# Attention and an MLP on one core: W1 loads in 2 KB rows, and a batch's head transposes moved from TensorE to DMA

## Chip, cores and metric

The kernel runs on one core of one Trainium2 chip. The metric is the device time of one execution in microseconds. Before the change the median of three runs is 740.92 us (740.89 to 741.25).

## What is computed

Grouped-query attention (8 batches, 16 query heads on 4 key/value heads, 384 tokens, head size 64) gives x of 384 x 1024 per batch. A residual MLP with affine norms follows:

```
scores = scale * q @ k^T;  attn = softmax(scores);  x = attn @ v      (heads side by side)
a1  = alpha1 * x + beta1
u   = x + lam * (w_tok @ a1)
a2  = alpha2 * u + beta2
out = u + lam * (relu(a2 @ w_ch1) @ w_ch2)        w_ch1: 1024 x 4096, w_ch2: 4096 x 1024
```

## The kernel before

**Stages.** Batch 0's attention runs first (`side(0)`). Then `main(0)` runs the MLP of batch 0, and the attention of batch 1 is woven into it; `main(1)` runs the MLP of batch 1 with the attention of batch 2. These two are the plain passes. Then `pair(0)` to `pair(2)` run the MLPs of the other six batches two by two, with sums and differences of blocks in place of some of the products. The attention of each later batch is woven into the stage ahead of it.

**The order is written by hand.** All five instruction streams are in the order in which the program calls them (`manual_schedule`, L836). `main` and `pair` are generators: they yield 0 in the first matrix product and 1 in the second, and the driver (L1011 to L1026) counts these units and calls what `put(ps, phase, unit, ...)` has planned for each. A plan entry therefore fixes a place in each engine's own order. An engine waits only for semaphores of data that it needs, or of a buffer that must be free.

**First product of a plain pass** (L524 to L547). W1 is taken in 16 chunks of 256 columns (`CW` = 2 column tiles of 128) over all 1024 rows of K. They go through a ring of `RING` = 6 slots in SBUF. `load_w1` (L183) issues one transfer from GpSimd's queue (POOL), which also casts f32 to bf16: 1 KB source rows, 512 KB written. `order1` is 0, 8, 1, 9, 2, 10, ...; batch 1 goes through it backwards. For each column tile `nt` there are eight matmuls (L531) over `dt`, the eight parts of K. Then ACT or VectorE (DVE) applies bias and ReLU and writes `hT` (L540, L542); `exps`, set by the exponentials (L290), decides which of the two does it. When a chunk's two tiles are done its slot is freed and the chunk six places on is loaded (L545). PSUM has two banks for these products. In batch 0 the first four column tiles (`FIRST`: 0, 1, 16, 17) are computed early, inside `side(0)` (`h_part`, L223), since `a2` is not complete yet.

**W2** is held whole in SBUF during the plain passes. Three of its sixteen parts (512 KB, 2 KB source rows, L189) are loaded early and 13 after batch 0's last W1 load (L549), all on POOL's queue. Behind them come the keys, queries and values of batch 2 (`load_next(2)`). POOL has at most eight transfers under way. The second product (L569) goes over the column tiles in the order of the first; the first two output tiles are each run to three quarters before they are finished.

**Heads.** Attention needs q and k with head dimension on partitions. For batch 1 TensorE transposes them (`k_transpose` L255, `q_transpose` L265) at units 9, 24, 28, 32, 36 and 40 of `main(0)`'s first product, and DVE copies the result out of PSUM (L257, L267). For batches 2 to 7 DMA transposes issued from SP do it (`flip_k` L172, `flip_q` L176). `kT` and `qT` have one buffer each, and so have the raw keys (`k2s`) and queries (`qrs`).

**The other parts that the prediction's steps touch.** On SP: rows of parameters (`load_row_set`, L924), the spill of x (L243), the transposes of `a2` (L362), and the stores of batch 0 (L518). On PE: the scores (L279, three calls at a time in `scores3`), attention times values (L315) and token mixing (L340). `scores3(0)` of batch 1 stands at unit 0 of `main(0)`'s second product and reads the keys and the queries of heads 0 to 3. `late` holds back the last exponential of some `scores3` until after the next `av` (L408).

**The end** (L767 to L796, `last` and `o == 4`). The last of seven products goes through the first half of its 16 K parts for token tiles 0, 1, 2 and then through the second half for 0, 1, 2. Token tile 2 is in two PSUM pieces, 384 and 128 columns wide. Two DVE operations on each finished piece (L794, L795) and a store from SP (L796) follow.

Of the kernel before, what the change touches and what calls it, by code (L numbers as in the profile page):

```python
# [12 lines left out]
def kernel(  # L13
# [21 lines left out]
    nc = tc.nc  # L35
# [13 lines left out]
    P = 128  # L49
# [7 lines left out]
    CW = 2  # L57
# [57 lines left out]
    def by_tok(ap):  # L115
        return ap.rearrange("(p st) d -> p st d", st=NST)
# [64 lines left out]
    w1_slots, w1_free = {}, list(range(RING))  # L181

    def load_w1(c):  # L183
        w1_slots[c] = w1_free.pop(0)
        nc.gpsimd.dma_start(out=w1[:, w1_slots[c]], in_=w1src[:, :, c * CW * P:(c + 1) * CW * P])  # L185

    def load_w2(dw, r, h):
        cs = slice(dw * 512, (dw + 1) * 512)
# [23 lines left out]


    early = {}
    FIRST = (0, 1, NH, NH + 1)

    def h_part(nts, dts):
        for nt in nts:
            if nt % 2 == 0 and nt not in early:
                t = bank([P, 2, 512], "sc", "h")  # L220
                early[nt], early[nt + 1] = t[:, 0], t[:, 1]
            for dt in dts:
                nc.tensor.matmul(out=early[nt][:, :S + 1], lhsT=w1[:, w1_slots[nt // CW], dt, nt % CW * P:(nt % CW + 1) * P],  # L223
                                 rhs=a2Ts[0][:, dt, :S + 1], start=(dt == 0), stop=(dt == NDT - 1))


# [2 lines left out]
    def side(b):  # L229
# [175 lines left out]
        def av(p):  # L405
            av_piece(p, 0)
            av_piece(p, 1)
            while late:  # L408
                late.pop(0)()

        def tok_flip(p):
            tok(p)
# [18 lines left out]
        if not first:  # L431


            turns = {}
            if b == 1:
                turns = {5: [(to_all, 3, 0, 0), (load_row_set, 1, 1, 0)], 7: [(to_all, 3, 1, 1), (load_row_set, 2, 0, 1)],
                         9: [(k_transpose, 0)], 12: [(to_all, 1, 0, 2)], 14: [(to_all, 1, 1, 0), (load_row_set, 2, 1, 0)],
                         17: [(scale_beta,)], 20: [(to_all, 2, 0, 1)], 22: [(to_all, 2, 1, 0)],
                         24: [(q_transpose, 0, 2, "av")], 28: [(k_transpose, 2)]}
                for i in range(3):  # L440
                    turns[32 + 4 * i] = [(q_transpose, 2 + 2 * i, 2, "av")]
            if (b - NPL) // 2 > 0:
                at = {}

                def put(k, *m):
                    at.setdefault(k, []).append(m)

                for j in range(6):
                    put((0, 6, 12, 21, 26, 31)[j], scores3, j, j in (2, 5))
                for p in range(NP):  # L450
                    put((4, 10, 14, 18, 24, 29, 33, 35)[p], av, p)
                    put((8, 15, 17, 22, 27, 32, 36, 38 if b % 2 else 39)[p], tok_flip, p)
                    if by_pe(p):
                        put((36, 39, 41)[p - NP + 3], turn, p)
                return turns, at
            return turns, {
                0: [(scores3, 0)], 4: [(av, 0)], 6: [(scores3, 1)], 8: [(tok_flip, 0)], 11: [(av, 1)],
                13: [(scores3, 2, True)], 15: [(av, 2)], 16: [(tok_flip, 1)], 18: [(tok_flip, 2)], 19: [(av, 3)],
                21: [(scores3, 3)], 23: [(tok_flip, 3)], 25: [(av, 4)], 27: [(scores3, 4)], 29: [(tok_flip, 4)],
                31: [(av, 5)], 33: [(scores3, 5, True)], 35: [(av, 6), (tok_flip, 5)], 37: [(av, 7)],  # L460
                38: [(tok_flip, 6)], 41: [(tok_flip, 7)],
                **{39 + 4 * i - i // 2 * 2: [(turn, p)] for i, p in enumerate((5, 6, 7)) if by_pe(p)}}
# [20 lines left out]
            for f, *a in at.get(i, []):  # L483
                add(f, *a)
        for f, *a in ((tok, 4), (ut, 3), (h_part, (0, 1), range(3)), (av, 7), (a1, 7), (tok, 5), (ut, 4), (h_part, (0, 1), (3,)),
                      (tok, 6), (h_part, (16, 17), range(4)), (ut, 5), (tok, 7), (h_part, FIRST, (4,)), (ut, 6),
                      (h_part, FIRST, (5,)), (ut, 7), (h_part, FIRST, (6,)), (h_part, FIRST, (7,))):
            add(f, *a)
        return us
# [18 lines left out]
            f(**a)  # L508


    order1 = [c for g in range(NCH // 2) for c in (g, g + NCH // 2)]

    def store(b, ms, dw, o):
# [6 lines left out]
    def main(b):  # L520
        a2T = a2Ts[b]
        n = S + 1 if b == 0 else S

        seq = order1[::-1 if b % 2 else 1]  # L524
        for i, c in enumerate(seq):
            for j in range(CW):
                nt = c * CW + j
                begun = b == 0 and nt in early
                ps = early[nt] if begun else bank([P, 512], "mm", "h")
                for dt in range(0 if begun else NDT):  # L530
                    nc.tensor.matmul(out=ps[:, :n], lhsT=w1[:, w1_slots[c], dt, j * P:(j + 1) * P],  # L531
                                     rhs=a2T[:, dt, :n], start=(dt == 0), stop=(dt == NDT - 1))
                    if dt == 3:
                        yield 0
                c1 = bias1[:, nt:nt + 1]
                if b == 0:
                    evac("DVE" if nt % 2 else "ACT")(out=c1, in_=ps[:, S:n])
                exps[0] -= 1
                if (b or nt % 2 == 0) and exps[0] < 0:
                    nc.scalar.activation(out=hT[:, nt, :], in_=ps[:, :S], func=RELU, bias=c1)  # L540
                else:
                    nc.vector.tensor_scalar(out=hT[:, nt, :], in0=ps[:, :S], scalar1=c1,  # L542
                                            scalar2=0.0, op0=ADD, op1=mybir.AluOpType.max)
                yield 0
            if i + RING < NCH:  # L545
                w1_free.append(w1_slots.pop(c))
                load_w1(seq[i + RING])  # L547

            if b == 0 and i == NCH - RING:  # L549
                for dw, r, h in [(0, 1, 1)] + [(0, r, h) for r in (2, 3) for h in range(2)] + [  # L550
                        (1, r, h) for r in range(4) for h in range(2)]:
                    load_w2(dw, r, h)
                load_next(2)
        nts = [c * CW + j for c in seq for j in range(CW)]
        units = [(dw, ms) for dw in range(NDW) for ms in range(NST)]
        runs = [(k, 0, NNT) for k in range(len(units))]
        if b == 0:
            most = 3 * NNT // 4
            runs[:2] = [(k, lo, hi) for lo, hi in ((0, most), (most, NNT)) for k in range(2)]
        open_ps = {}  # L560
        for k, lo, hi in runs:
            dw, ms = units[k]
            cs = slice(dw * 512, (dw + 1) * 512)
            if lo == 0:
                open_ps[k] = bank([P, 512], "mm", "ch")
            ps = open_ps[k]
            for i in range(lo, hi):
                nt = nts[i]
                nc.tensor.matmul(out=ps, lhsT=hT[:, nt, ms * P:(ms + 1) * P],  # L569
                                 rhs=w2[:, row(nt)[0], row(nt)[1], cs], start=(i == 0), stop=(i == NNT - 1))  # L570
                if i % 4 == 3 and i < NNT - 1:
                    yield 1
            if hi < NNT:
                continue
            o = obuf[:, k % 2 * 512:(k % 2 + 1) * 512]
            nc.vector.tensor_tensor(out=o, in0=ps, in1=lam_t[:, cs], op=MUL)
            if b == 0:
                nc.vector.tensor_tensor(out=o, in0=o, in1=xs[0][:, ms, cs], op=ADD)
            store(b, ms, dw, o)
            yield 1  # L580
# [89 lines left out]
    def pair(i):  # L670
# [95 lines left out]
        where = {2: (0, 0), 3: (0, 1), 7: (1, 1), 4: (1, 0)}  # L766
        for k, o in enumerate(PLACE2):  # L767
            whole = not last and o != 4
            for h in range(1 if whole else 2):
                for ms in range(NST):  # L770
                    if o == 4 and not last and 1 < 3 * h + ms < 5:
                        sum_w1(0, (5, 7, 6)[3 * h + ms - 2])
                    if last and (o, h) in ((6, 1), (7, 0)):
# [7 lines left out]
                        X[ms] = c_banks(ms)  # L781
                        pairs["held"] = ms == NST - 1
                    upto = NH if whole else 8 * h + 8
                    for (c0, c1, x), t in ((c, t) for c in X[ms] for t in range(8 * h, upto)):
                        slot, rhs = w2_slots[i, 4 * k + t // 4], w2_at[i, 4 * k + t // 4]
                        nc.tensor.matmul(out=x, lhsT=hid[:, t, LEFT2[o], ms * P:(ms + 1) * P],  # L786
                                         rhs=rhs[:, t % 4 * 512 + c0:t % 4 * 512 + c1],
# [4 lines left out]
                        if last and o == 4 and t == NH - 1:  # L792
                            e, v = ends[ms][:, c0:c1], spare(ms).bitcast(f32)[:, c0:c1]
                            tt(out=v, in0=x, in1=lam_t[:, c0:c1], op=MUL)  # L794
                            tt(out=e, in0=e, in1=v, op=ADD)  # L795
                            nc.sync.dma_start(out=by_tok(out[b0 + 1])[:, ms, c0:c1], in_=e)  # L796
                        if t % 4 == 3 and t < upto - 1 and c1 == 512:
                            q = 4 * ms + t // 4
                            if whole and o in (2, 6) and q in (2, 5, 8, 10):
# [36 lines left out]
    with tc.manual_schedule(engines=order):  # L836
# [104 lines left out]
        nc.gpsimd.dma_start(out=wtok_in, in_=moe_w_tok.rearrange("(p tt) s -> p tt s", tt=NST))  # L941
        load_q4(3)
        place_k(0, 0, (0,))
        load_w1(order1[0])
        load_w1(order1[1])
        place_k(0, 1)
        scale_rows(1, nc.gpsimd)
        split(1, 2, None, nc.gpsimd)
        for c in order1[2:RING]:
            load_w1(c)  # L950

        load_q(1)
# [27 lines left out]
        turns, at = side(1)  # L980
        put_all(0, 0, turns)
        put_all(0, 1, at)
        put_flips(0, 1, 2, (34, 36, 37, 42, 43))

        put(0, 1, 45, load_next, 3)
# [71 lines left out]
```

## Time and profile before

| what | value |
|---|---|
| runs | 740.92 us median (740.89, 740.92, 741.25) |
| profiled execution | 740.56 us |
| its span, first to last instruction | 738.8 us |
| mean granted TensorE clock | 0.999 |
| TensorE (PE) busy | 731.5 us, 99% |
| VectorE (DVE) busy | 516.9 us, 70% |
| ScalarE (ACT) busy | 324.1 us, 44% |
| GpSimd (POOL) busy | 163.5 us, 22% |
| queue q0 (POOL's transfers) | 64.60 MB |
| queue q1 (SP's transfers) | 85.39 MB |

The profile gives one execution, in microseconds from the span's first instruction. Each group of instructions has its line, engine, operation and tiles; "idle before" is the time in which its engine did nothing ahead of it, with what ended that. The chain of work follows the last instruction back to what released it, step by step. The DMA view gives the packets and bytes of each queue, for the span or for a window of it; sizes are those written. The time to landing of a transfer is counted from its issue.

### The profile page before, as it was taken

Reading aid. Unit: us, or ns where it says so; the run is one execution under the profiler, and the core shown is the slowest. Engines: PE = TensorE matmul, PEld = TensorE weight load, DVE = VectorE, ACT = ScalarE, POOL = GpSimd, SP = SyncE. Lnnn points to the kernel's source line nnn. Section 1 sums busy time; section 2 is a strip of 40 time slices with the busy share of each in tenths; the row PEclk is TensorE's granted clock in tenths of the full one; section 3 lists DMA queues with packets and bytes.
Section 4 is the critical chain, followed back from the end, with each engine's and each line's share of the span. In section 5 each row is a group of like instructions: output and inputs, shape, how many; then the busy total and the mean of one; then the engine's idle time right before and its main releaser. Section 6 shows DMA issues by size and latency. Waiting matters only on the chain.

```text
span 738.8 us, 14511 instructions
## 1 busy us (share of the span) xinstructions
PE 731.5 (99%) x5769; PEld 418.8 (57%) x5769; DVE 516.9 (70%) x995; ACT 324.1 (44%) x467; POOL 163.5 (22%) x211
## 2 busy tenths in 40 slices
PE   8999999999999999999999999999999999999997
PEld 5866555566555566655555566655555566654444
DVE  7763366467587889749777988847968988762354
ACT  7632431444333566653334366664343266660000
POOL 9434221420000232211013244020002222000011
PEclk9999999999999999999999999999999999999999
DMA  9999999999899999999989999998989999937965
GB/s 184 194 202 200 207 209 175 185 191 199 204 258 281 177 218 212 268 249 205 297 197 197 202 149 191 204 246 198 274 236 172 211 127 145 172 117 261 293 182 103
DMA packets 218017, 151.32 MB, mean 205 GB/s; under 512 B 88660, under 2 KB 197060, under 8 KB 217948
## 3 DMA queue, kind: packets, MB, share of 16 engines
q0 software_dynamic: 120304, 64.60, 66.6%
q1 hardware_dynamic: 97100, 85.39, 42.9%
q8 instruction: 45, 0.74, 0.4%
q10 hardware_dynamic: 544, 0.39, 0.2%
q14 instruction: 24, 0.20, 0.1%
HBM read 154.84 MB, written 38.27 MB: 261 GB/s over the span
## 4 chain that ended last, share of the span: by engine, by line
PE 95%; DVE 2%; DMA 1%; ACT 0%; issue 0%; DVEq 0%
PE C L786 30%; PE X L722 17%; PE h L531 10%; PE ch L569 10%; PE Y L722 8%; PE sc L279 5%; PE Z L722 4%; PE sc L315 4%; PE sc L340 3%; DMA ops<-a 1%; PE h L223 1%; PE tok L340 1%; PE av L315 0%; PE warm L841 0%; PE tp L265 0%; ACT hT L288 0%
## 5 line engine op out<-in xcount | busy, mean ns | idle before, releaser
L288 ACT ACTIVATE es<-sc 128x1024 bf16<-128x1024 f32 x126 | 121.4, 1023 | 155.9 <-PE sc L279 144.8
L786 PE MATMUL C<-w,arena 128*128 128x512 bf16 (+2 forms) x744 | 168.0, 372 | 0.0
L786 PEld LDWEIGHTS <-arena 128*128 128x128 bf16 x1040 | 94.8, 98 | 100.5 <-issue 5.1
L727 ACT ACTIVATE hT<-X,bias 128x384 f32<-128x384 f32 x144 | 83.7, 581 | 61.6 <-PE X L722 54.9
L722 PEld LDWEIGHTS <-w 128*128 128x128 bf16 x768 | 75.1, 98 | 50.0
L516 POOL DMA_DIRECT2D out_dram<-hT x33 | 28.7, 871 | 284.3 <-DVE hT L687 106.3
L569 PE MATMUL ch<-arena,hT 128*128 128x512 bf16 x384 | 90.8, 379 | 0.0
L185 POOL DMA_DIRECT2D w<-in_moe_w_ch_dram x68 | 62.8, 964 | 98.4 <-PE X L722 34.4
L531 PE MATMUL h<-ops,w 128*128 128x384 bf16 (+1 forms) x480 | 83.3, 327 | 0.8 <-DVE hT L542 0.7
L722 PEld LDWEIGHTS <-pad 128*128 128x128 bf16 x576 | 56.4, 98 | 37.2
L722 PE MATMUL X<-ops,w 128*128 128x384 bf16 x384 | 70.2, 326 | 0.0
L722 PE MATMUL X<-ops,pad 128*128 128x384 bf16 x384 | 70.2, 326 | 0.0
L786 PE MATMUL C<-pad,arena 128*128 128x512 bf16 (+2 forms) x296 | 69.9, 373 | 0.0
L531 PEld LDWEIGHTS <-w 128*128 128x128 bf16 x480 | 45.4, 98 | 30.4 <-issue 2.7
L569 PEld LDWEIGHTS <-hT 128*128 128x128 bf16 x384 | 34.8, 98 | 36.8 <-issue 2.5
L347 DVE TENSOR_TENSOR xr<-sc,xr 128x384 f32<-128x384 f32 x56 | 30.9, 552 | 23.4 <-PE sc L340 23.4
L315 PEld LDWEIGHTS <-es 128*128 128x128 bf16 x1008 | 38.2, 97 | 12.4
L340 PEld LDWEIGHTS <-wtokT 128*128 128x128 bf16 x576 | 37.5, 98 | 11.8 <-DVE a L330 0.8
L279 PE MATMUL sc<-qT,kT 64*128 64x384 bf16 (+2 forms) x576 | 42.0, 272 | 0.8 <-DVE xr L323 0.3
L320 DVE RECIPROCAL rinv<-sc 128x6 f32<-128x6 f32 x56 | 10.7, 192 | 44.3 <-PE sc L315 44.1
L315 PE MATMUL sc<-v,es 128*128 128x65 bf16 x1008 | 39.8, 193 | 0.0
L722 PE MATMUL Z<-ops,w 128*128 128x384 bf16 x192 | 39.0, 326 | 0.0
(138 smaller groups left out, 911.0 us busy)
## 6 DMA issues: line engine op xcount, KB each, us to landing
w<-in_moe_w_ch_dram POOLq DMA_DIRECT2D x68, 512.0 KB, 10.3
w<-w2s SPq DMA_DIRECT2D x60, 512.0 KB, 4.3
pad<-w2s SPq DMA_DIRECT2D x24, 512.0 KB, 8.1
out_dram<-xr SPq DMA_DIRECT2D x56, 192.0 KB, 6.1
out_dram<-hT POOLq DMA_DIRECT2D x33, 256.0 KB, 5.7
arena<-in_moe_w_ch_dram POOLq DMA_DIRECT2D x16, 512.0 KB, 20.0
w2s<-arena SPq DMA_DIRECT2D x28, 256.0 KB, 5.0
q_raw<-in_q_dram POOLq DMA_DIRECT2D x28, 192.0 KB, 10.4
```

The costliest lines, as they stand in the source:

```text
L185: nc.gpsimd.dma_start(out=w1[:, w1_slots[c]], in_=w1src[:, :, c * CW * P:(c + 1) * CW * P])
L279: nc.tensor.matmul(out=sc[:, hh, k % 4:k % 4 + n], lhsT=kT[r, 2 * p // G, BLK[hh][sk], :], rhs=qT[r, p, st:st + n, :], start=True, stop=True)
L288: nc.scalar.activation(out=e, in_=sc, func=EXP, scale=scale_qk)
L315: nc.tensor.matmul(out=av[:, hh, sq, :], lhsT=ess[k // 4][:, m % 2, k % 4, :], rhs=vb[:, sk, hk, :], start=(sk == 0), stop=(sk == NST - 1))
L340: nc.tensor.matmul(out=ps[:, tt, :], lhsT=wtokT[:, st, tt * P:(tt + 1) * P], rhs=a1s[p][:, st, :], start=(st == 0), stop=(st == NST - 1 an ...
L347: nc.vector.tensor_tensor(out=u, in0=ps, in1=u, op=ADD)
L516: nc.gpsimd.dma_start(out=at, in_=o, accum_op=ADD)
L531: nc.tensor.matmul(out=ps[:, :n], lhsT=w1[:, w1_slots[c], dt, j * P:(j + 1) * P], rhs=a2T[:, dt, :n], start=(dt == 0), stop=(dt == NDT - 1))
L569: nc.tensor.matmul(out=ps, lhsT=hT[:, nt, ms * P:(ms + 1) * P], rhs=w2[:, row(nt)[0], row(nt)[1], cs], start=(i == 0), stop=(i == NNT - 1))
L722: nc.tensor.matmul(out=ps, lhsT=tb[g, o][:, dt, e * P:(e + 1) * P], rhs=opb(LEFT1[o])[:, dt], start=(o in (1, 2, 7) and dt == 0), stop=(dt ...
L727: nc.scalar.activation(out=snap[o, e], in_=ps, func=IDENT, bias=hi if o == 5 else lo)
L786: nc.tensor.matmul(out=x, lhsT=hid[:, t, LEFT2[o], ms * P:(ms + 1) * P], rhs=rhs[:, t % 4 * 512 + c0:t % 4 * 512 + c1], start=((not last o ...
```

## The change

1. In batch 0, and in the first half of batch 1, W1 is taken in chunks of 512 columns over half of K's rows: 2 KB source rows, again 512 KB written, in the same six slots. Four column tiles now use two slots (`half`, `w1_of`), and both are freed and loaded again after the four. `order0` is column group 0, 4, 1, 5, 2, 6, 3, 7, each with its two halves of K. Batch 1 goes through groups 7, 3, 6, 2 and then through chunks 11, 3, 10, 2, 9, 1, 8, 0 of the old form. `FIRST` becomes 0, 1, 2, 3. The 13 loads of W2 and `load_next(2)` stand after 20 column tiles and not after 22.
2. Batch 1's keys and queries are transposed by DMA: `flip_k(1)` and two `flip_q` at units 50, 54, 58 of `main(0)`'s first product, two more at units 3 and 9 of its second. TensorE's six groups of transposes are gone.
3. After held-back exponentials have run, `exps` is 1 and not 2.
4. At the end, token tile 2 is left out of the first half and run over all 16 K parts last; the store of its 128-column piece is issued by ACT.

```diff
     def load_w1(c):
-        w1_slots[c] = w1_free.pop(0)
-        nc.gpsimd.dma_start(out=w1[:, w1_slots[c]], in_=w1src[:, :, c * CW * P:(c + 1) * CW * P])
+        w1_slots[c] = slot = w1_free.pop(0)
+        if isinstance(c, tuple):
+            src = w1src[:, c[1] * NDT // 2:(c[1] + 1) * NDT // 2, c[0] * 512:(c[0] + 1) * 512]
+            nc.gpsimd.dma_start(out=half(slot), in_=src)
+        else:
+            nc.gpsimd.dma_start(out=w1[:, slot], in_=w1src[:, :, c * CW * P:(c + 1) * CW * P])
+
+    def half(slot):
+        return w1[:, slot].rearrange("p a c -> p (a c)").rearrange("p (a c) -> p a c", a=NDT // 2)
+
+    def w1_of(nt, dt):
+        g = nt // 4, dt // (NDT // 2)
+        if g in w1_slots:
+            return half(w1_slots[g])[:, dt % (NDT // 2), nt % 4 * P:(nt % 4 + 1) * P]
+        return w1[:, w1_slots[nt // CW], dt, nt % CW * P:(nt % CW + 1) * P]
...
-    FIRST = (0, 1, NH, NH + 1)
+    FIRST = (0, 1, 2, 3)
...
             while late:
                 late.pop(0)()
+                exps[0] = 1
...
-                         9: [(k_transpose, 0)], 12: [(to_all, 1, 0, 2)], 14: [(to_all, 1, 1, 0), (load_row_set, 2, 1, 0)],
-                         17: [(scale_beta,)], 20: [(to_all, 2, 0, 1)], 22: [(to_all, 2, 1, 0)],
-                         24: [(q_transpose, 0, 2, "av")], 28: [(k_transpose, 2)]}
-                for i in range(3):
-                    turns[32 + 4 * i] = [(q_transpose, 2 + 2 * i, 2, "av")]
+                         12: [(to_all, 1, 0, 2)], 14: [(to_all, 1, 1, 0), (load_row_set, 2, 1, 0)],
+                         17: [(scale_beta,)], 20: [(to_all, 2, 0, 1)], 22: [(to_all, 2, 1, 0)]}
...
-                      (tok, 6), (h_part, (16, 17), range(4)), (ut, 5), (tok, 7), (h_part, FIRST, (4,)), (ut, 6),
+                      (tok, 6), (h_part, (2, 3), range(4)), (ut, 5), (tok, 7), (h_part, FIRST, (4,)), (ut, 6),
...
+    order0 = [(q + h, i) for q in range(4) for h in (0, 4) for i in range(2)]
...
-        seq = order1[::-1 if b % 2 else 1]
-        for i, c in enumerate(seq):
-            for j in range(CW):
-                nt = c * CW + j
+        seq = order1[7::-1] if b else order0
+        if b:
+            seq = [(q, i) for q in (7, 3, 6, 2) for i in range(2)] + seq
+        to_load, nts = seq[RING:], []
+        for c in [c for c in seq if c not in order0 or not c[1]]:
+            mine = [(c[0], 0), (c[0], 1)] if c in order0 else [c]
+            for nt in range(4 * c[0], 4 * c[0] + 4) if c in order0 else range(CW * c, CW * c + CW):
+                nts.append(nt)
...
-            if i + RING < NCH:
-                w1_free.append(w1_slots.pop(c))
-                load_w1(seq[i + RING])
-
-            if b == 0 and i == NCH - RING:
+            fresh = bool(to_load)
+            for m in mine if fresh else ():
+                w1_free.append(w1_slots.pop(m))
+                load_w1(to_load.pop(0))
+
+            if b == 0 and fresh and not to_load:
...
+            tail = last and o == 4
             for h in range(1 if whole else 2):
-                for ms in range(NST):
+                for ms in range(NST - (tail and not h)):
...
-                    for (c0, c1, x), t in ((c, t) for c in X[ms] for t in range(8 * h, upto)):
+                    for (c0, c1, x), t in ((c, t) for c in X[ms]
+                                           for t in range(0 if tail and ms == NST - 1 else 8 * h, upto)):
...
-                            nc.sync.dma_start(out=by_tok(out[b0 + 1])[:, ms, c0:c1], in_=e)
+                            (nc.scalar if c0 else nc.sync).dma_start(out=by_tok(out[b0 + 1])[:, ms, c0:c1], in_=e)
...
-        load_w1(order1[0])
-        load_w1(order1[1])
+        load_w1(order0[0])
+        load_w1(order0[1])
...
+        put_flips(0, 0, 1, (50, 54, 58))
+        put(0, 1, 3, flip_q, 1, 4, 2)
+        put(0, 1, 9, flip_q, 1, 6, 2)
```

More of the change, by code (lines that the diff above doesn't have):

```diff
@@ L222, in h_part @@
             for dt in dts:
-                nc.tensor.matmul(out=early[nt][:, :S + 1], lhsT=w1[:, w1_slots[nt // CW], dt, nt % CW * P:(nt % CW + 1) * P],
+                nc.tensor.matmul(out=early[nt][:, :S + 1], lhsT=w1_of(nt, dt),
                                  rhs=a2Ts[0][:, dt, :S + 1], start=(dt == 0), stop=(dt == NDT - 1))
@@ L530, in main @@
                 for dt in range(0 if begun else NDT):
-                    nc.tensor.matmul(out=ps[:, :n], lhsT=w1[:, w1_slots[c], dt, j * P:(j + 1) * P],
+                    nc.tensor.matmul(out=ps[:, :n], lhsT=w1_of(nt, dt),
                                      rhs=a2T[:, dt, :n], start=(dt == 0), stop=(dt == NDT - 1))
@@ L553, in main @@
                 load_next(2)
-        nts = [c * CW + j for c in seq for j in range(CW)]
         units = [(dw, ms) for dw in range(NDW) for ms in range(NST)]
@@ L948 @@
         split(1, 2, None, nc.gpsimd)
-        for c in order1[2:RING]:
+        for c in order0[2:RING]:
             load_w1(c)
```

## The prediction

> **What bounds the kernel now.** First the page's engine and chain lines:
>
> ```profile
> span 738.8 us, 14511 instructions
> PE 731.5 (99%) x5769; PEld 418.8 (57%) x5769; DVE 516.9 (70%) x995; ACT 324.1 (44%) x467; POOL 163.5 (22%) x211
> PE 95%; DVE 2%; DMA 1%; ACT 0%; issue 0%; DVEq 0%
> ```
>
> TensorE is the bound nearly everywhere, at a granted clock of 1.00 in every stage. A matmul removed from it is time won, and a wait added to it is time lost. The waits of PE come to 3.2 us in the whole span, and none of them is for a transfer:
>
> ```profile
> PE warm L841 <- DVE wtokT L844: 1.5, 1, 1.5
> PE h L531 <- DVE hT L542: 0.7, 1, 0.7
> ...
> ```
>
> That PE does not wait for transfers does not mean that transfers have room. The table of stages gives the DMA share above 1.2 from 10 to 130 us, so I read the DMA view in three windows there: 50 to 60 us (W1 in 1 KB source pieces, 512 B written), 72 to 84 us (W2 in 2 KB pieces, 1 KB written), and 93.5 to 95.5 us (W2 beside a DMA transpose from SP).
>
> ```profile
> DMA packets 3898, 1.98 MB, mean 198 GB/s; under 512 B 60, under 2 KB 3896, under 8 KB 3896
> ```
> ```profile
> DMA packets 2480, 2.48 MB, mean 206 GB/s; under 512 B 76, under 2 KB 2479, under 8 KB 2479
> ```
> ```profile
> q0 software_dynamic: 315, 0.31, 92.1%
> q1 hardware_dynamic: 313, 0.08, 29.9%
> ```
>
> W1 moves at 198 GB/s and W2 at 206: the load queue is saturated and the piece size is worth 4%. In the third window the two queues share the engines packet by packet, 315 to 313. So a transpose, in packets of 256 B (0.08 MB / 313), lets W2 through at 157 GB/s, 76% of its rate.
>
> **Slack of the W1 loads.** Number batch 0's sixteen loads in order of issue. Loads 7 to 16 are issued at 36.84 to 59.41 us; adding each one's time to landing, they land at 46.6, 49.3, 52.1, 54.8, 57.3, 60.1, 62.7, 65.4, 68.0, 70.6, one per 2.67 us. W2's next seven land one per 2.55 us, from 70.6 to 85.9. The PE timeline gives the consumption:
>
> ```profile
> 40.63 0.50 PE L255 MATMUL tp<-ident,k 128*128 128x128 bf16 x6
> 40.96 9.96 PE L531 MATMUL h<-ops,w 128*128 128x385 bf16 x60
> 50.76 0.50 PE L265 MATMUL tp<-ident,q_raw 128*128 128x128 bf16 x6
> ```
>
> Sixty matmuls take 50.76 - 40.96 = 9.80 us, 163 ns each, 1.31 us for a column tile of eight. L531 begins at 36.71, so load 7 is needed at 36.71 + 8 x 1.31 + 0.33 = 47.5 (landed 46.6), load 8 at 50.1 (49.3), load 16 at 72.6 (70.6). The slack is 0.8 to 2 us: PE is fed just in time.
>
> **Part 1, the second batch's heads.** Gone from PE: 2 groups on L255 and 4 on L265 of six transposes, each group 40.96 - 40.63 = 0.33 us: **-1.97 us**, all on the path. Their six VectorE copies of 0.55 us go too and are worth nothing, as DVE idles before each L537 there. Added on SP: one flip_k and four flip_q. SP works in its own order and each waits only for its data. Ahead of them stands the last row load of the first stage:
>
> ```profile
> 41.34 4.36 SPq L924 DMA_DIRECT2D rows<-in_moe_alpha_dram  x2
> ```
>
> The keys of batch 1 are converted by 36.4 (L160), the queries have landed by 35, and kT and qT were last read for batch 0 before 27 us. So the places 50, 54 and 58 in the plan hold nothing back: flip_k and the first three flip_q are issued from 45.8 on, one after another. The row load issued by 45.7 reached DVE at 49.73 (its shuffle L928 waited for it), so I let the flips' first packets move at 50 us. They carry 12 + 3 x 6 = 30 blocks of 128 x 128 in bf16, 32 KB or 128 packets each: 3840 packets at 157 per us, 24.5 us, until 74.5. Over that time the loads' spacing grows from 2.55 to 2.55 x 206 / 157 = 3.34 us. The flips themselves are in time: flip_k ends at 59.8, then 64.7, 69.6, 74.5, and the first scores come with the second matmul product after 75. The fourth flip_q stands on SP behind the first spill (86.64) and T of L362 (87.38, landed after 9.3), some 13 us before its scores (107.8).
>
> **Part 2, W1 in halves of four column tiles.** The loads gain (2.67 - 2.55) each, so load 7 lands 7 x 0.12 = 0.8 to 0.9 earlier, at 45.7. But four tiles now need two loads: loads 7 and 8 are both wanted at tile 20, at 36.71 + 8 x 1.31 = 47.2 and, for the second half of K, 4 x 0.163 later, 47.8. Before, load 8 was wanted at 50.1. It lands at 45.7 + 2.55 = 48.25: a new wait of 0.47, even without flips. With flips (3.34 from 50 us on) loads 10, 12, 14, 16 land at 53.9, 60.6, 67.2, 73.9; wanted, each 5.23 + the waits so far after the one before, at 53.5, 59.2, 65.8, 72.5. **Waits: 0.47 + 0.43 + 1.43 + 1.43 + 1.43 = 5.2 us**, all on PE, with nothing to hide them: the products of W1 are all that PE has there. What is queued behind the waiting matmul on PE is the whole rest of the kernel. Loads are issued by POOL after the last reader of a slot, two at a time; load 15 can be issued at 58.7 and would move at 66, so issue is not the limit. POOL's time per load falls (0.87 to about 0.74, as L189's same shape), hidden.
>
> [...]
>
> W2 behind: its loads land some 3.7 us later. The tightest (columns 0 to 511, rows 8 to 11, second half of NNT) landed at 78.3 and becomes 82; the second product starts 3.2 later, at 78.5, and now wants it after its 20th matmul, which stood 81.03 - 75.30 = 5.7 after the start: 84.2. No wait. If PE did not slip, it would be wanted at 79.5 and be there at 78.3 - 16 x 0.12 = 76.4: 3 us of cover. The later flip_q takes 768 packets, 5 us at 76%, 1.2 us off the second half of W2, whose last part lands at 108.5 and is read near 112.
>
> Batch 1's pass: only halves (2,0) and (2,1) are loaded in the new form. (2,1) takes the place of the 8th load, landed 153.0 (148 to 152 moved 118 GB/s at its worst); it is now wanted at 152.7 instead of 154.7, and its predecessor and itself are 4% faster and meet a spill with 1 KB packets (141 to 110 GB/s before). 0, bounded by 0 and +0.7.
>
> **Part 3, exps[0] = 1.** It gives the second ReLU after a held-back exponential to ACT (idle 4.28 us before 182.8) instead of DVE. The wait it could touch, 0.66 us at 181.3 for L542, is for the first such ReLU, which stays on DVE (started 180.65). 0; bounds -0.7 and 0.
>
> **Part 4, the end.** The same matmuls, other order. Before, DVE's last four operations stand in a queue: 734.62, 735.21, 735.68, 736.00 + 0.29. Now the 384-wide part is ready 16 x 0.054 = 0.87 before PE's end, not 0.43, at about 734.3, so the four start at 734.3, 734.9, 735.4, 735.7 and end at 736.0. The last store is issued by ACT, but SP was free too (its four issues take 0.34 each). **-0.3**, bounds -0.8 (as if DVE's whole tail went) and +0.3 (a first issue on ACT that is slower by its SP duration).
>
> **Sum.** -1.97 + 5.2 - 0.3 = **+2.9 us**. The profiled run took 740.56 (span 738.78 and 1.78 around it), giving 743.5; it lies 0.36 under the median of 740.92, so **743.8 us**.
>
> **Rivals.**
> 1. *The flips do not slow the loads* (faster). Against it stands 315 to 313 packets; for it, that this window is one transpose of three blocks, and flip_k is four times as long. Then only load 8's 0.47 stays: 740.92 - 1.97 + 0.47 - 0.3 = 739.1, or 738.6 if load 8 is in time too. It decides where the spacing under flips stays below 2.65; at about 2.85 the gain and the waits cancel.
> 2. *Half of it*: spacing near 2.9, waits of about 2.4, 741.0.
> 3. *The flips are held until their places in the plan* (unit 50 is PE at 64). Then packets move at 68, the 18 blocks of the keys and the first queries take 2304 / 157 = 14.7 and land at about 84.2 (1.5 from last packet to landing), and the first scores, wanted at 74.7, wait 9.5: about 748. Against it: nothing that SP waits for is that late.
> 4. *W1 gains nothing from 1 KB pieces*: load 7 at 46.6, the others 2.67 and then 2.67 x 206 / 157 = 3.50 apart, waits of 1.5 + 1.1 + 1.8 + 1.8 + 1.7 = 7.8, 740.92 - 1.97 + 7.8 - 0.3 = 746.4. Against it: the rates of the two windows. [...]
> Within the forecast lies a pause of all queues such as that at 150 to 151 us (windows down to 27 GB/s during a transpose): one in the stage adds about 1.2.
>
> **Numbers.** 0.2% is about what a measurement of this kernel tells from no change (1.5 us: 739.4 to 742.4). Forecast: 0.60, its own range 742.4 to 745.5. Rival 1: 0.22, of which 0.02 ends inside 0.2%. Rival 2: 0.10. Rival 3: 0.05. Rival 4: 0.03. Faster 0.20, same 0.12, slower 0.68. The range 738.4 to 746.0 leaves out rivals 3 and 4, some 0.06 of the forecast above it and 0.04 of rival 1 below it.
>
> **What would show it.** Right: PE h waits for DMA w in four or five places of 0.4 to 1.5 us between 47 and 73, each before the fifth matmul of a first tile; SP's DMA_TRANSPOSE of kT at about 46; q0 at about 157 GB/s from 50 to 74; second product starting near 78.5 instead of 75.3. Wrong: no such wait and a start at 73.3 to 73.8 (rival 1), or scores waiting for qT (rival 3). At the end, DVE's last operation should close 0.3 nearer to PE's last matmul.

## The result, and the profile after

The changed kernel takes 751.69 us (median of six runs, 748.53 to 752.39), the kernel before 740.82 beside it (740.31 to 741.25). The ratio is 1.0135, with a 95% interval of 1.0115 to 1.0156: 10.9 us slower, 7.9 above the 743.8 predicted and 5.7 above the range. The profiled execution after took 748.90 us; a second profile of the same kernel (after_again, below) took 746.97 and helps to take the loss apart. Runs of the changed kernel differ by up to 3.9 us among themselves; the granted clock of TensorE differs too and explains a part of it, as the experiments show.

The page's engine and chain lines, after:

```profile
span 747.1 us, 14381 instructions
PE 727.9 (97%) x5674; PEld 416.9 (56%) x5733; DVE 510.7 (68%) x987; ACT 325.7 (44%) x469; POOL 161.5 (22%) x211
PE 78%; DMA 7%; issue 6%; DVE 5%; POOL 4%; ACT 0%; POOLq 0%; DVEq 0%
```

The busy time of PE in this profile can't be set against the one before: 59 of its matmuls have no record (5674, but 5733 weight loads). In after_again, where all 5733 are recorded, PE is busy for 729.7 us, 1.8 less than before, close to the 1.97 of the transposes that are gone. The chain that was 95% PE is 78% PE here and 86% in after_again; the rest is DMA, VectorE, POOL and "issue", which is time for which the profile shows no wait. The list of PE's waits says where time is lost:

```profile
PE h L547 <- DMA w<-in_moe_w_ch_dram: 5.7, 4, 2.1
PE sc L292 <- DVE xr L336: 2.2, 1, 2.2
...
PE Y L738 <- DVE arena L751: 0.9, 1, 0.9
```

Before, no wait was for a transfer. Now four are, 5.7 us in all, and one wait for VectorE's xr has grown from 0.3 to 2.2. To see what they cost, measure PE's stages from start to start, since a wait can hide in work that is stretched (us; a stage ends where the next one's first matmul starts):

| stage | before | after | after_again |
|---|---|---|---|
| up to batch 0's second product | 75.30 | 81.53 | 80.42 |
| batch 0's second product | 55.70 | 57.57 | 57.95 |
| batch 1's first product | 56.52 | 55.78 | 55.78 |
| batch 1's second product | 55.55 | 55.56 | 55.55 |
| first product of pair(1) | 72.80 | 73.93 | 72.80 |
| from pair(2)'s second product to the end | 76.56 | 76.36 | 76.32 |

The other stages are equal within 0.02. The sums are +8.3 and +6.4 us. The 1.1 in pair(1) is in one execution of this kernel and not in the other. Of the experiments below with W1 in halves, e1, e3, e7 and e10 show 0.79 to 1.42 there and e5 and e6 nothing; those with W1 in the old pieces show 0 to 0.54. Whether this is the change's stays open.

**The first product** shows the predicted mechanism. PE's timeline, with the idle time and its releaser in brackets:

```profile
49.72 3.59 PE L547 MATMUL h<-ops,w 128*128 128x385 bf16 x21
54.45 5.40 PE L547 MATMUL h<-ops,w 128*128 128x385 bf16 x32 [1.14 <-DMA w<-in_moe_w_ch_dram]
61.07 5.40 PE L547 MATMUL h<-ops,w 128*128 128x385 bf16 x32 [1.22 <-DMA w<-in_moe_w_ch_dram]
67.76 5.40 PE L547 MATMUL h<-ops,w 128*128 128x385 bf16 x32 [1.29 <-DMA w<-in_moe_w_ch_dram]
75.26 6.43 PE L547 MATMUL h<-ops,w 128*128 128x385 bf16 x28 [2.10 <-DMA w<-in_moe_w_ch_dram]
```

A wait every 32 matmuls (four column tiles), at their fifth matmul, where the second half of K is wanted. The flips, the DMA transposes of the heads, go out where they were forecast (SP's timeline), and the DMA view of 50 to 74.5 us shows what they take:

```profile
45.37 4.34 SPq L172 DMA_TRANSPOSE kT<-k  x1
49.81 15.30 SPq L176 DMA_TRANSPOSE qT<-q_raw  x3
```
```profile
q0 software_dynamic: 3704, 3.68, 91.6%
q1 hardware_dynamic: 3716, 0.93, 31.1%
```

3704 packets of loads went to 3716 of flips, one to one. The loads got 3.68 MB in 24.5 us, 150 GB/s. In the same window of the profile before they had the engines nearly to themselves and got 4.87:

```profile
q0 software_dynamic: 8568, 4.87, 140.3%
```

The last line of PE's timeline hides something else. Its 28 matmuls take 6.43 us, and in after_again 4.75. The table of windows of 1 us has the granted clock as the third number from the right:

```profile
74.00:75.00 1.00, 0.00 (x0) 0.00 (x0) 0.00 (x0) 0.00 (x0) 0.00 (x0) 1.00 1.23 199
75.00:76.00 1.00, 0.74 (x3) 0.36 (x4) 0.00 (x0) 0.00 (x0) 0.50 (x1) 0.75 1.25 198
76.00:77.00 1.00, 1.00 (x5) 0.48 (x4) 0.00 (x0) 0.39 (x2) 0.24 (x1) 0.50 1.27 210
77.00:78.00 1.00, 1.00 (x5) 0.48 (x4) 0.00 (x0) 0.35 (x1) 0.00 (x0) 0.50 1.23 205
78.00:79.00 1.00, 1.00 (x5) 0.48 (x4) 0.00 (x0) 0.00 (x0) 0.74 (x1) 0.54 1.24 206
```

Right behind the wait the clock is halved. What is missing from 1.00 in the four windows is 0.25 + 0.50 + 0.50 + 0.46 = 1.71 us lost, so the stretch at half speed was twice that, 3.4 us.

**The second product** loses 1.9 to 2.3 us, which the prediction did not have. SP's timeline, then VectorE's, first after and then before:

```profile
94.95 2.46 SPq L176 DMA_TRANSPOSE qT<-q_raw  x1
98.74 2.80 SPq L530 DMA_DIRECT2D out_dram<-obuf  x2
...
106.28 4.27 SPq L375 DMA_TRANSPOSE ops<-a  x1
```
```profile
100.00 1.98 SPq L362 DMA_TRANSPOSE ops<-a  x1
```
```profile
110.42 0.69 DVE L592 TENSOR_TENSOR obuf<-ch,vecs 128x512 f32<-128x512 f32 x1 [3.15 <-DMA out_dram<-obuf]
...
115.50 0.56 DVE L364 TENSOR_TENSOR a<-xr,vecs 128x384 bf16<-128x384 f32 x1 [3.19 <-DMA ops<-a]
```
```profile
103.39 0.69 DVE L576 TENSOR_TENSOR obuf<-ch,vecs 128x512 f32<-128x512 f32 x1 [2.35 <-PE ch L569]
...
107.39 0.56 DVE L351 TENSOR_TENSOR a<-xr,vecs 128x384 bf16<-128x384 f32 x1 [2.12 <-DMA ops<-a]
```

The last flip_q (94.95) goes ahead of stores and of the transposes of `a2` on the same queue. One of these now takes 4.27 us to issue and not 1.98. VectorE waits 3.15 us for a store to free `obuf`, where it waited 2.35 for PE, and 3.19 for a transpose, where it waited 2.12. Counted from the start of the stage, the two operations come 0.80 and 1.88 later than before (28.89 for 28.09, 33.97 for 32.09). So xr is late, and PE's scores wait 2.19 for it at 116.8; at 108.7, the same place before, they waited 0.30.

### The profile page after: what moved, and what is told of

The parts are those of the page before. It is cut to its first block, busy times and chain, and to the rows that moved or that the text cites. A ratio compares the mean times of both kernels' runs of the same rounds, so it can differ in the third digit from the quotient of the medians.

```text
span 747.1 us, 14381 instructions
## 1 busy us (share of the span) xinstructions
PE 727.9 (97%) x5674; PEld 416.9 (56%) x5733; DVE 510.7 (68%) x987; ACT 325.7 (44%) x469; POOL 161.5 (22%) x211
## 4 chain that ended last, share of the span: by engine, by line
PE 78%; DMA 7%; issue 6%; DVE 5%; POOL 4%; ACT 0%; POOLq 0%; DVEq 0%
PE C L804 26%; PE X L738 14%; PE ch L585 10%; PE Y L738 7%; PE h L547 6%; DMA w<-in_moe_w_ch_dram 6%; PE sc L292 4%; PE sc L328 4%; PE Z L738 3%; PE sc L353 3%; DMA ops<-a 1%; POOL w L187 1%; DVE xr L336 1%; DVE a1f L341 1%; DVE xr L360 0%
## 5 line engine op out<-in xcount | busy, mean ns | idle before, releaser
L804 PE MATMUL C<-w,arena 128*128 128x512 bf16 (+2 forms) x711 | 163.7, 372 | 1.6 <-issue 0.3
L585 PE MATMUL ch<-arena,hT 128*128 128x512 bf16 x366 | 87.9, 379 | 1.0 <-issue 0.3
L189 POOL DMA_DIRECT2D w<-in_moe_w_ch_dram x50 | 46.9, 993 | 83.5 <-PE X L738 38.7
L738 PE MATMUL Y<-ops,w 128*128 128x384 bf16 x192 | 39.0, 326 | 0.9 <-DVE arena L751 0.9
```

The lines of the kernel that those rows point to most:

```text
L189: nc.gpsimd.dma_start(out=w1[:, slot], in_=w1src[:, :, c * CW * P:(c + 1) * CW * P])
L738: nc.tensor.matmul(out=ps, lhsT=tb[g, o][:, dt, e * P:(e + 1) * P], rhs=opb(LEFT1[o])[:, dt], start=(o in (1, 2, 7) and dt == 0), stop=(dt ...
```

## Theories and experiments

Theory: the packets of the flips are the cause, in the first product by slowing W1, in the second by standing on SP's queue; on top of the waits comes the clock. There are three rivals. The halves of K's rows, two loads due at one tile, could make the waits by themselves. W2 that comes late could make those of the second product. The clock could fall for a reason of its own. The experiments ran on several chips, so each time stands beside that of the kernel before on the same chip.

**Undo the flips** (e1, against the changed kernel).

```diff
-                         12: [(to_all, 1, 0, 2)], 14: [(to_all, 1, 1, 0), (load_row_set, 2, 1, 0)],
-                         17: [(scale_beta,)], 20: [(to_all, 2, 0, 1)], 22: [(to_all, 2, 1, 0)]}
+                         9: [(k_transpose, 0)], 12: [(to_all, 1, 0, 2)], 14: [(to_all, 1, 1, 0), (load_row_set, 2, 1, 0)],
+                         17: [(scale_beta,)], 20: [(to_all, 2, 0, 1)], 22: [(to_all, 2, 1, 0)],
+                         24: [(q_transpose, 0, 2, "av")], 28: [(k_transpose, 2)]}
+                for i in range(3):
+                    turns[32 + 4 * i] = [(q_transpose, 2 + 2 * i, 2, "av")]
...
-        put_flips(0, 0, 1, (50, 54, 58))
-        put(0, 1, 3, flip_q, 1, 4, 2)
-        put(0, 1, 9, flip_q, 1, 6, 2)
```

> The changed kernel with the second batch's heads turned by TensorE again, as before; W1 in halves, exps[0] = 1 and the new end stay. Theory (the flips' packets slow the loads, and the late W1 halves are what PE waits for): no wait for w of 0.5 us or more in the first product, the clock stays at 1.00, and the time is 740.8 - 0.74 (the wait that exps[0] took away) - 0.18 (end) = 739.9. Rival (halves of K's rows make two loads due at one tile, which costs the waits without any flip): waits for w at loads 10, 12, 14 and 16 of more than 1 us each stay, and the time is 745 or more. Between the two, the one wait of 0.47 that the prediction gave load 8 without flips would make 740.4.

Measured: 739.88 us (12 runs; before on that chip 740.12; ratio 0.9992, 0.9979 to 1.0004), mean clocks 0.999 to 1.000. The only wait for w left, in its list of waits:

```profile
PE h L550 <- DMA w<-in_moe_w_ch_dram: 0.3, 1, 0.3
```

It is at 48.0 us, load 8, where the prediction put 0.47 for a kernel without flips. The first rival falls: with the halves and without the flips the time is that of the kernel before. The first product ends at 75.17, 0.13 before the old one. One of the 23 runs of the kernel before on that chip took 744.64 us at a mean clock of 0.997, so the clock can fall without the change too; no trace of that run shows why.

**Only the flips** (e2: before, with the flips in the same places and the six groups gone from PE; W1 in its old pieces).

> The kernel before with the flips alone (same places as in the change, and TensorE's six groups gone): W1 in the old pieces of 512 B written, exps and the end as before. Theory (the flips' packets are the cause, whatever the pieces of W1): beside packets of 512 B a flip leaves the load queue 120 of 198 GB/s (that is what the loads moved beside flips at 441 to 446 us of the kernel before), 3840 packets at 240 per us last 16 us and cost the loads 6 us, of which their slack takes up about 2: waits for w of about 4 us in all, the wait of 2.2 us for xr at 117 as in the changed kernel, so 744 to 746, and up to 749 where the clock falls. Rival (the halves are what turns a slower queue into waits): waits for w under 1 us and a time under 742.

Measured: 751.07 us (749.51 to 752.86, 4 runs; before 740.58), ratio 1.0139 (1.0122 to 1.0157): as much as the whole change loses, from the flips alone. It falls in other places, though. In the profile the first product ends 3.5 us later than before (5.1 in after_again, with the halves) and the second takes 5.4 longer (2.3). The DMA view of 53 to 65 us, then its waits:

```profile
q0 software_dynamic: 2893, 1.46, 88.6%
q1 hardware_dynamic: 2887, 0.71, 47.4%
```
```profile
PE h L528 <- DMA w<-in_moe_w_ch_dram: 4.9, 5, 1.7
PE sc L279 <- DVE xr L323: 3.9, 1, 3.9
```

One to one again, so packets of 512 B leave the loads 1.46 MB / 12 us = 122 GB/s and 1 KB packets left them 150; the flips are done sooner in return (2887 / 12 = 241 packets per us here, 3716 / 24.5 = 152 there). W1's waits are 4.9 us where 4 were expected, the one at 116 is 3.9 where 2.2 was, and a stretch at half clock (1.7 us) follows it. The time is above the 749 given as the most.

**Fewer flips** (e10, against the changed kernel): the keys flipped early, the queries on PE.

```diff
-                         17: [(scale_beta,)], 20: [(to_all, 2, 0, 1)], 22: [(to_all, 2, 1, 0)]}
+                         17: [(scale_beta,)], 20: [(to_all, 2, 0, 1)], 22: [(to_all, 2, 1, 0)],
+                         24: [(q_transpose, 0, 2, "av")]}
+                for i in range(3):
+                    turns[32 + 4 * i] = [(q_transpose, 2 + 2 * i, 2, "av")]
...
-        put_flips(0, 0, 1, (50, 54, 58))
-        put(0, 1, 3, flip_q, 1, 4, 2)
-        put(0, 1, 9, flip_q, 1, 6, 2)
+        put(0, 0, 50, flip_k, 1)
```

> The changed kernel with only the keys of batch 1 flipped early (12 blocks, 1536 packets); the queries are turned by PE as before. Theory (the loss grows with the packets that meet W1's loads): 1536 / 157 = 9.8 us at 76% cost the loads 2.3 us, their slack takes up 0.5 to 1, so waits for w of 1.3 to 1.8 us in the first product, against 6.9 with 24 blocks; two PE groups of 0.33 are gone; 739.9 - 0.66 + 1.3 to 1.8 = 740.5 to 741.1, and the clock stays at 1.00. Rival (a flip beside the loads costs a fixed pause, or the whole form is what waits): waits of 4 us or more and 743 or more.

(The change has 30 blocks there, not the 24 of that text.) Measured: 742.36 us (741.33 to 742.88; before 740.36), above the theory's 740.5 to 741.1 and below the rival's 743. The waits for w are 2.8 us, against 0.3 without flips and 6.9 in after_again. Per block of 128x128 that is 2.5 / 12 = 0.21 and 6.6 / 30 = 0.22 us: two points in proportion, and no sign of a fixed price. The theory's mechanism holds; the slack of 0.5 to 1 us that I allowed the loads is not there. A block turned by PE costs 0.33 / 6 = 0.055 us.

**Move the last flip_q ahead** (e3, against the changed kernel).

```diff
-        put(0, 1, 9, flip_q, 1, 6, 2)
+        put(0, 1, 3, flip_q, 1, 6, 2)
```

> The changed kernel with its last flip_q put at plan place 3 of the second product instead of 9, so that SP issues it ahead of the transposes of the first token tile. Theory (the late flip holds those transposes on SP, VectorE waits for them and PE's scores for VectorE): the wait of PE of 2.2 us at 116.8 goes back under 0.5, the second product of batch 0 takes 55.7 us again, and the time falls by 1.9. Rival (the loss is W2 that comes late behind the transposes' packets): the wait stays or moves to W2's tile w, and the time stays within 0.5 of the changed kernel's.

```profile
PE h L547 <- DMA w<-in_moe_w_ch_dram: 6.8, 5, 2.2
...
PE sc L292 <- DVE xr L336: 0.5, 1, 0.5
```

The wait of the scores is 0.5 and the second product takes 55.90 us. The time is 746.78 (745.36 to 747.47; before 740.12): 6.7 above before and not 10.9, so 4.2 were won and not the 1.9 expected. Its four runs had mean clocks of 0.999 to 1.000, the changed kernel's 0.994 to 0.998 in ten of eleven. So, by the mean clocks, moving this flip also took away the stretches at half clock, though the five waits for w stayed (the largest 2.20). The second rival falls: the wait went with the flip's place on SP. A new wait of 0.71 for a transpose of `a2` stands in batch 1's first product, which takes 56.65; its cause is not shown.

**What the clock follows.** First the changed kernel again (after_again):

> The changed kernel once more, for the two groups in which its times fell (748.5 to 748.9, and 751.6 to 752.4). Theory (the groups differ in how many stretches of about 3.4 us at half clock follow the waits at 75 and 117 us, each 1.7 us dear): times near 752 go with mean clocks of 0.995 to 0.996 and, where the profile falls among them, it shows two such stretches; times near 748.7 go with one, 0.998. Rival (the groups differ in waits): the mean clocks of both groups are alike and the profile of a slow one shows a longer wait somewhere.

The profiled run took 746.97 us at a mean clock of 1.000, with waits for w of 6.9 us and one of 2.57 for xr, and no stretch at half clock. The four others took 750.89 to 751.86 at 0.994 to 0.995. 0.005 of 745 us is 3.7 us, 0.006 is 4.5: 746.97 + 3.7 to 4.5 = 750.7 to 751.4. The clock accounts for most of the gap between them. It does not for the two groups of the first six runs (748.9 and 748.53 at 0.998 and 0.997; 751.55 to 752.39 at 0.995 to 0.998). The six profiles of this case with one stretch have mean clocks of 0.997 and 0.998, so by that scale five of those six runs had one stretch each, and still they lie 3.9 us apart. There the theory is not borne out, and what else differs stays open.

Then the four waits for w of the first profile were filled with matmuls that nothing uses (e7, against the changed kernel):

```diff
+    FILL = {8: 7, 24: 7, 12: 7, 28: 11}
...
+                    if b == 0 and dt == 4 and nt in FILL:
+                        fill = bank([P, 512], "av", "fill")
+                        for _ in range(FILL[nt]):
+                            nc.tensor.matmul(out=fill[:, :S], lhsT=wtokT[:, 0, :P], rhs=wtokT[:, 1, :],
+                                             start=True, stop=True)
```

> The changed kernel with 32 more matmuls of 128x384 that compute nothing that is used (7, 7, 7 and 11 of them), put into the four places where PE waits for a half of W1, so that PE is busy there. They take about 1.1 to 1.8 us in each place, no more than the waits. If the idle time is what drops the granted clock to 0.50 at 75 to 78.5: the clock stays at 1.00 there, the second product begins 1.5 to 1.8 earlier, and the time falls by as much. If the clock falls for another reason: it falls here too, and the time is that of the changed kernel or up to 1 us longer.

Measured: 750.76 us (750.38 to 751.51; before 740.12), mean clocks 0.995 to 0.998. The clock stayed up at 76 us (the 28 matmuls there took 4.74 us) and the second product began at 80.58, but in after_again it began at 80.42 with nothing filled, so the profile decides nothing. The second product took 60.03 us, 4.33 longer than before: its wait for xr was 2.9 and not 0.3, and the 1.7 left is what a stretch of half clock takes. The time did not fall: inconclusive on the first product, and a pointer to the wait for xr.

So a single wait was put into the kernel before, which has none of 2 us or more (e11):

```diff
+        def stall():
+            t = sb.tile([P, 6], f32, tag="stall", name="stall", bufs=1)
+            nc.vector.memset(t, 1.0)
+            for _ in range(12):
+                nc.vector.reciprocal(out=t, in_=t)
+        put(0, 1, 11, stall)
```

> The kernel before with twelve small operations put on VectorE (12 x 0.19 us, nothing of them is used) ahead of the one for which PE's scores wait at 108.7 us: one wait of about 2.6 us on PE, and nothing else changed. Theory (one wait of more than 2 us is enough for a stretch of about 3.4 us at half clock, in most executions): the time rises by 2.3 for the wait and by 1.7 more, to 744.6, the mean clock falls to 0.997 or 0.998, and the profile shows 0.50 right behind the wait. Rival (several waits close together are needed): 742.9 at a mean clock of 1.000.

740.79 us (before 740.36; ratio 1.0006, 0.9997 to 1.0015) at mean clocks of 0.999 to 1.000. Place 11 is at 88 us, where VectorE had time to spare, and PE did not wait for it. So the operations alone do not lower the clock; of a wait this run says nothing. At place 25, with 12 (e12) and with 18 operations (e13):

> As e11_one_stall, with the twelve operations moved to where they do hold PE: right ahead of the VectorE operations for whose xr PE's scores wait at 108.7 us. One wait of about 2.6 us. Theory (one wait of more than 2 us is enough in most executions): mean clock 0.997 or 0.998 in most of them, the time 2.3 + 1.7 above before, 0.50 right behind the wait in the profile. Rival (several waits near each other are needed, or a longer one): 2.3 above before at a mean clock of 0.999 to 1.000.

> As e12_stall_2p6 with eighteen operations: one wait of about 3.8 us. [...] If single waits do not matter: 3.5 above before. If 2.6 is enough already, both show the 1.7.

e12: 744.15 us (before 740.58), +3.6, and a mean clock of 0.998 in all four runs. PE's timeline before, then that of e12 and its windows:

```profile
108.70 0.39 PE L279 MATMUL sc<-qT,kT 64*128 64x128 bf16 x4 [0.30 <-DVE xr L323]
109.03 1.90 PE L569 MATMUL ch<-arena,hT 128*128 128x512 bf16 x8
```
```profile
110.84 0.39 PE L279 MATMUL sc<-qT,kT 64*128 64x128 bf16 x4 [2.86 <-DVE xr L323]
111.17 3.23 PE L569 MATMUL ch<-arena,hT 128*128 128x512 bf16 x8
```
```profile
111.00:112.00 1.00, 1.00 (x7) 0.36 (x4) 0.93 (x2) 0.67 (x1) 0.74 (x1) 0.79 1.31 216
112.00:113.00 1.00, 1.00 (x4) 0.38 (x3) 0.00 (x0) 0.36 (x1) 0.00 (x0) 0.50 1.40 191
113.00:114.00 1.00, 1.00 (x4) 0.36 (x3) 0.00 (x0) 0.00 (x0) 0.00 (x0) 0.50 1.91 67
114.00:115.00 1.00, 1.00 (x9) 0.81 (x8) 0.00 (x0) 0.00 (x0) 0.00 (x0) 0.51 1.48 173
```

One wait of 2.86 us, then eight matmuls in 3.23 us that took 1.90 before; 0.21 + 0.50 + 0.50 + 0.49 = 1.70 lost. The second product is 59.96 - 55.70 = 4.26 longer, 2.56 of wait and 1.70 of clock. In e13 the wait broke into 0.96 and 2.33 us, 4 us apart, so it did not test a wait of 3.8. Its median is 744.2 us; two of its four runs show 0.997 and two 0.999 to 1.000, and the profile, one of the former, has a stretch behind the 2.33. One wait of 2.9 us is enough, then, and the third rival falls for this place; 2.1 to 2.6 did it in some profiles and not in others.

**Flips, but held** until W1 is loaded, by an in-place copy of one column by VectorE that the plan's unit 50 releases: 18 blocks (e5), then 12 (e6). The edit for 12, against e1 (for 18, half of the keys are held, flipped and taken from PE alike):

```diff
-                for i in range(3):
-                    turns[32 + 4 * i] = [(q_transpose, 2 + 2 * i, 2, "av")]
+                turns[32] = [(q_transpose, 2, 2, "av")]
...
+        def hold():
+            c = qrs[1][:, 8:, 0, :1]
+            nc.vector.tensor_copy(out=c, in_=c)
+        put(0, 0, 50, hold)
+        for i in (4, 6):
+            put(0, 0, 50, flip_q, 1, i, 2)
```

> The kernel e1_no_flips with three of the six groups (18 blocks of 128x128) given to flips that are truly held until the end of W1's loads: a copy of one column in place by VectorE, which PE's 50th unit (about 64 us) releases, stands between the data and flip_k and two flip_q. Theory: the flips then meet W2, which has 3 us of cover, and three groups of 0.33 us are gone from PE: no wait for w in the first product, and 739.9 - 1.0 = 738.9. Rival (W2's cover is not enough): waits for w of 1 us or more in the second product, and 740 to 741.

> As e5_18_held with two of the groups (12 blocks, two flip_q) held and the rest on PE. Theory: 739.9 - 0.66 = 739.2, no wait for w. Rival: the flips cost the second product 0.5 us or more of waits and nothing is left of the gain, 739.9 or more.

Both theories fell, and the times lie above the rivals' as well: 743.59 us (742.06 to 744.95) and 741.94 (741.35 to 745.29; before 740.58). In e5's profile, the fastest of its runs, the first product is 1.08 shorter, as expected of three groups, with no wait for w of note, and then these follow:

```profile
PE ch L587 <- DMA arena<-in_moe_w_ch_dram: 1.4, 1, 1.4
PE h L549 <- DMA ops<-a: 0.6, 1, 0.6
PE sc L292 <- DMA qT<-q_raw: 0.5, 1, 0.5
```

W2 is late by 1.4 us at 112.5: its cover of 3 us was not enough. All six runs of e5 have mean clocks of 0.999 or 1.000, so what its slower ones lose, up to 2.9 us, is not the clock; it is not shown. e6's profile fell on its slowest run (waits for w of 0.84 and 2.36 us in batch 1, and a stretch at half clock behind them); what its usual runs lose is not shown.

**The parts that pay.** `exps[0] = 1` alone (e4), then with the new end (e9):

> The kernel before with exps[0] = 1 alone. If the wait of PE for VectorE's hT before batch 1's first product (0.66 us at 181.3) is what it takes away: that wait is gone and the time is 740.1, 0.7 below before. If the 0.74 that the changed kernel gained in that segment came from the order of the W1 pieces: no change, 740.8.

> The kernel before with exps[0] = 1 and the new end of the last token tile, and nothing else of the change. Theory: the gains of the two add, 0.66 and 0.2 us, so 0.86 below the kernel before on the same chip (ratio 0.9988), and below e4_exps_only by 0.2. Rival (the end's gain is lost again, by the store that ACT now issues): as e4_exps_only, 0.7 below.

739.45 us against 740.12 (ratio 0.9988, 0.9977 to 0.9999), and 739.73 against 740.36 (0.9993, 0.9984 to 1.0002). In both the 0.66 wait for hT is gone from the list; at its place the same product now waits 0.17 and 0.18 for w. The end of e9 is 76.32 and not 76.56, 0.24 shorter, but two waits for w of 0.8 us together (the 0.18 among them) stand against it. e4's ratio is the lowest here, 0.1% below before; the intervals of e4, e9 and e1 overlap, so their order is not shown.

## Why the prediction was wrong, by its steps

- **Sharing of the queues: right.** 3704 to 3716 packets over 24.5 us, as 315 to 313 had said; about 155 GB/s for the loads in undisturbed microseconds (157 forecast); SP's flips at 45.4, last packets at 75.5 (74.5).
- **Waits of W1: right in place and kind, too small.** Forecast 5.2 us in five waits; 6.9 in after_again (five, 1.16 to 1.72 each), and 80.42 - 75.30 + 1.97 = 7.1 from start to start. The terms too small are "0.43" for load 10 (1.14 and 1.47 in the two profiles) and "0.47" for load 8 (0 and 1.22). In the first profile load 10 came 0.5 later than forecast (54.45, not 53.9) and was wanted 0.2 earlier (53.3, not 53.5). Load 16's wait, 2.10 and 1.72, contains in both profiles the pause of all queues that the forecast held possible (45 GB/s for 0.6 us near 70.5 in the first; 134 and 108 GB/s in the microseconds from 70 and 71 in after_again, 197 to 206 beside them).
- **"The later flip_q takes 768 packets ... 1.2 us off the second half of W2": this failed.** W2 made no wait in either profile. I asked whether the flip was in time for its scores and what it took from W2, and not who stands behind it on SP. Transposes and stores did, VectorE behind them, and PE: +1.9 and +2.3 us, of which 0.2 is left in e3_flip_early. It is the question that I did ask for PE's queue.
- **"A wait added to it is time lost": true, but not one for one.** I read a clock of 1.00 in every stage and carried it over to a kernel with waits. Each stretch at half clock costs 1.70 us more. In after_again 4 to 5 us lie between the run with none and the others; the first six runs, by their mean clocks, had one stretch each and in one case two.
- **exps: 0 forecast, 0.74 gained in that stage** (-0.7 was its bound). The product that had waited 0.66 starts at 188.68 in the profile after, right when ACT's ReLU ends (188.05 + 0.58) and while VectorE's still runs, so it gets the PSUM bank that ACT frees. I had tied the wait to the first ReLU alone.
- **End: -0.3 forecast, -0.20 and -0.24.** Batch 1's pass and W2: 0 forecast, no wait in either profile.

From 743.8: W1's waits 7.1 instead of 5.2 (+1.9), the second product (+2.3), exps (-0.7), the end (+0.1) give 747.4; after_again's run without a stretch took 746.97. One stretch (1.7) leads to 749.1, where the two faster of the first six runs are (748.5 and 748.9). The other 2.6 us up to the median of 751.7 stay open: a second stretch could account for 1.7, but the mean clock speaks for it in one of the six runs only. Rival 3's 748 was nearer by luck: it is a sum for flips that are held, and none was; no run shows its 1.5 us from last packet to landing, and the transpose issued at 87.38 in the profile before landed at 96.7, 0.4 to 0.7 after its last packets. (Rival 4's five waits add up to 7.9 and not 7.8, which moves its time by 0.1.) The range ended at 746.0 because every case in it was a case of the first product, each wait priced at its own length.

## What to carry over

Price a transfer that moves beside a saturated queue by its packets and not by its bytes (here 3716 packets of 0.93 MB moved for 3704 of 3.68 MB), against the slack of whoever shares the engines. Then price it again by what stands behind it in the issuing queue (here 1.9 and 2.3 us). Here one block cost 0.22 us as a transfer and 0.055 on TensorE, the engine that was the bound. In a kernel that keeps PE busy for 99% of the time, as this one does, give a new wait of 2 us or more a bound of 1.7 us on top: six of nine such waits cost it here. Take several executions with their clocks before you read a difference of 2 us between two profiles as an effect.

## What the runs showed of the hardware

- The granted clock of TensorE fell to 0.50 for 3.4 us, behind some of its waits; 1.70 or 1.71 us were lost each time where windows of 1 us show it. The profiles hold nine waits of 2 us or more. Behind six there is such a stretch (2.10 in the first profile after, 2.33 in e13, 2.36 in e6, 2.86 in e12, 2.9 in e7, where the length of its stage tells it, 3.9 in e2), behind three there is none (2.19, 2.20 in e3, 2.57 in after_again). Behind shorter waits, up to 1.74, there is none. e12's mean clock was 0.998 in all four runs. The length of the wait alone does not decide: 2.10 had a stretch behind it and 2.57 had none. What else does is not shown.
- Where both queues had packets waiting they shared the engines packet by packet, in both pairs of sizes: 3704 to 3716 at 1 KB beside 256 B, 2893 to 2887 at 512 B beside 256 B.
- Issuing was slow too beside the saturated queue. SP needed 15.3 us to issue three transposes of 768 packets each, 151 packets per us, which is the rate at which flips' packets moved (3716 / 24.5 = 152). For one of `a2` it needed 4.27 us instead of 1.98.
